# An adaLN transformer block on one core: x's halves on one queue, a first norm in two chains, fill matmuls through the head, and a new issue order

## The chip, the core and the metric

The kernel runs on one core of a Trainium2 chip. A core has engines that each work through their own list of instructions in order: TensorE (PE, matmuls, with the weight loads shown apart as PEld), VectorE (DVE), ScalarE (ACT), GpSimd (POOL), and SyncE (SP), which here only issues transfers. Engines wait for each other by semaphores. The metric is the time of one execution in microseconds (us), lower is better.

## The reference

One transformer block on x of 2048 tokens by 512 features, in bfloat16, with modulation computed from a vector c:

```python
mod = (silu(c) @ w_mod).reshape(1, 6, 1, 512)          # sa, ca, ga, sb, cb, gb
h = layernorm(x) * (1 + ca) + sa
q, k, v = split(h @ wqkv)                              # 32 heads of 16
# token s attends to s, s-2, ..., s-14 (8 keys, positions below 0 masked)
o = softmax(q . k_gathered * 16**-0.5) @ v_gathered
x = x + ga * (o @ wo)
h = layernorm(x) * (1 + cb) + sb
x = x + gb * ((gelu(h @ w_gate) * (h @ w_up)) @ w_down)   # 1792 wide
```

## The kernel before, in words

The tokens are cut into four groups of 512 (`sg` 0 to 3), each of four tiles of 128 tokens on the partitions. For each group: layer norm (`LN1`), transpose to put features on the partitions (`hT`), the projections q, k, v (`qkv`, L562; each is four matmuls of 128 by 128 by 512 into one PSUM buffer, copied out by ScalarE, L576 to L582), the products q times shifted k on VectorE (`pq`, L617), their sums over features by TensorE (`lp`, L631, with a narrow stationary operand), the softmax on VectorE and ScalarE, the products with v (`pv`, L724), their sums (`o`, L738), the output projection (`x1p`, L759) with the residual (L768), the second norm (`LN2`), and the feed-forward part: gate and up (L787), gelu and copy on ScalarE, product on VectorE, and down (`y`, L799). v takes a way through DRAM (`vst`, `V4`), and some transposes go by a transfer (`LN1.3.t`, L463). PSUM has four buffers of the kind `mm`, two of the kind `att` and one for logits. `woS` (L368) and `WdS` multiply the weights wo and w_down by ga and gb on VectorE.

The order of all work is written out by hand as data. Every part of the kernel is a generator that yields steps (`Op`: an engine, a function that emits the instructions, the steps that must come before it, and buffers that it takes and gives). The generators are numbered in the order in which they are started, and the list `ORDER` says whose next step is emitted. So each engine's list of instructions follows `ORDER`; the waits between engines come from the data. The figures inside the steps were used when such a list was made and have no effect on a run.

The head of the kernel is this. x of the first group comes in two halves: tiles 0 and 1 on SP's queue (`x0.0`), tiles 2 and 3 on ScalarE's (`x0.2`, L260). Behind `x0.0` SP issues the weights of the modulation (`wm1`, `wm0`), then `wqkv0`, `x1`, `wqkv1`, `wqkv2`, `x2` and the rest. `mods` computes the modulation: silu of c on ScalarE (L316), a transpose (`scp`, L321), a copy (`scT`), a tiny exp that brings in the exp table (`pre`, L327), and two groups of sixteen matmuls with one column each (`mp1`, `mp0`, L293) whose results ScalarE turns into `scl` and `modT` (`mod1`, `mod0`). `mp3`, `mp4` (for the second norm) and `mp2`, `mp5` (for ga and gb) come later in the same way.

`norm` makes the first norm. Statistics of a tile are either two VectorE instructions (L407, L408; `st`) or, for the tiles in `ACT_CH`, ScalarE's: a copy with accumulation (`sa`, L385), a tiny scaling (`nm`, L391) and a square with accumulation (`sq`, L396). `rst` then adds the epsilon on VectorE (L433 for VectorE's tiles, L438 for ScalarE's) and raises to the power -1/2 on GpSimd (L444, `rs`), and L421 writes the normalized tile (`x0` to `x3`). Group 0 has no tile in `ACT_CH`, and its statistics form two parts (tiles 0 and 1, tiles 2 and 3) inside one generator, which emits all four statistics ahead of the first L421. `transp0` transposes each half on TensorE (`th0`, `th1`, L480), and ScalarE (L513) and VectorE (L511) apply the modulation and write `hT`. `qkv_halves` (L544) makes the first two q projections in halves of 256 tokens.

`warmup` emits twenty matmuls on zeros (L210), whose result nobody reads. In `ORDER` eight stand ahead of `scp`, five between `scp` and `mp1`, and seven between `th1` and the first half of L544.

Of the kernel before, what the change touches and what calls it, by code (L numbers as in the profile page):

```python
# [103 lines left out]
def kernel(  # L104
# [13 lines left out]
    nc = tc.nc  # L118
# [85 lines left out]
    def warmup(cold, n):  # L204
        yield Op("DVE", 0.25, lambda: nc.vector.memset(gB[:], 0.0), fire="warm")
        for k in range(n):
            def f(k=k):
                if k == 0:
                    B["warm"] = T("mm", [P, SG], F32, "warm_ps")
                nc.tensor.matmul(B["warm"][:], lhsT=gB[:, 0:P], rhs=gB[:], start=True, stop=True)  # L210
            yield Op("PE", 0.427 if k < cold else 0.216, f, after=["warm"], take=[SL["mm"]] if k == 0 else [],
                     give=[SL["mm"]] if k == n - 1 else [])

    def loads():
# [43 lines left out]
        def act_q():  # L258
            yield Op("ACT", 0.45, ldc, fire="c", lat=0.0, dma=True)
            yield Op("ACT", 0.46, ldx(0, 2, 4, nc.scalar), fire="x0.2", lat=1.45, dma=True)  # L260

        def sp_q():
            yield Op("SP", 0.47, ldx(0, 0, 2), fire="x0.0", lat=1.0)
            yield Op("SP", 0.47, ldwm(1), take=[SL["h2"]], fire="wm1", lat=3.2)
# [106 lines left out]
    ACT_CH = {"LN1.1": (3, 4), "LN1.2": (2, 4), "LN1.3": (0, 4), "LN2.0": (0, 2), "LN2.1": (0, 4)}  # L371
# [28 lines left out]
    def norm(key, src, ready, ev, parts=((0, 4),)):  # L400
        aa, ab = ACT_CH.get(ev, (0, 0))
        dv = [c4 for c4 in range(CPS) if not aa <= c4 < ab]
        for c4 in dv:
# [6 lines left out]
            for a, b in parts[:-1]:  # L410
                if c4 == b - 1:
                    yield from rst(ev, a, b, [c4 for c4 in dv if a <= c4 < b])
        a, b = parts[-1]
        yield from rst(ev, a, b, [c4 for c4 in dv if a <= c4 < b])
        for c4 in range(CPS):
            def f(c4=c4):
                k = norm_tiles(ev)
                if c4 == 0:
                    B[key] = T("xn", [P, CPS, D], BF16, "xn")
# [3 lines left out]
            yield Op("DVE", 0.325, f, after=[f"{ev}.rs{max(a for a, b in parts if a <= c4)}"],  # L423
# [96 lines left out]
    def ln1(sg):  # L520
        ev = f"LN1.{sg}"
        yield from norm(("xn1", sg), lambda: B["x", sg], lambda c4: [f"x0.{c4 // 2 * 2}"] if sg == 0 else [f"x{sg}"], ev,
                        ((0, 2), (2, 4)) if sg == 0 else ((0, 4),))
        pl.done[ev] = pl.done[f"{ev}.x3"]
# [12 lines left out]
    def qkv_halves():  # L537
        for half in range(2):
# [8 lines left out]
            yield Op("PE", 0.87, f, after=[f"LN1.0.h{d}.{half}" for d in range(DT)] + ["wqkv0"],  # L547
# [329 lines left out]
    pl.spawn(warmup(13, 20))  # L877
# [42 lines left out]
```

## Time and profile before

| | |
|---|---|
| Time, median of 3 runs | 242.76 us |
| Lowest and highest of the runs | 241.57 and 242.9 us |
| Span of the profiled execution, first to last instruction | 240.1 us |
| Whole time of the profiled execution | not given apart from its span |
| Busy: TensorE, VectorE, ScalarE, GpSimd | 233.0, 169.8, 152.8, 15.1 us |
| Moved by transfers | 29.68 MB |
| Mean granted TensorE clock | 0.993 of full |

The profile is a record of one execution: each instruction with its start and duration, the line of the kernel that emitted it, and what ended the idle time before it. Times in it are us from the span's start. "L787 PE MATMUL ... x224" groups the instructions of one line. A row of the chain gives start, duration, engine, tile and line. In a row of a window, each engine's busy time stands in the order TensorE, weight loads, VectorE, ScalarE, GpSimd, with counts in brackets; then the granted clock, the share of the transfer engines, and GB/s. TensorE's matmuls overlap, so its busy time says that it was occupied, not that it ran at its peak.

### The profile page before, as it was taken

How to read it: one execution, taken by the hardware profiler on the slowest of the kernel's cores; microseconds unless marked ns; L12 is line 12 of the kernel's file. 1: busy time of each engine (PE TensorE's matmuls, PEld its weight loads, DVE VectorE, ACT ScalarE, POOL GpSimd, SP SyncE). 2: the span in 40 equal slices, each digit the busy share in tenths (PEclk: the TensorE clock that was granted, in tenths of full speed). 3: DMA queues.
4: the chain of work that ended last, by engine and by line, in shares of the span. 5: the costliest groups of instructions: out<-in, count | busy, mean ns of one | idle time of the engine just before them, and what ended most of it. 6: DMA issues, size and time to landing. Idle time of an engine off the chain costs nothing.

```text
span 240.1 us, 3700 instructions
## 1 busy us (share of the span) xinstructions
PE 233.0 (97%) x1403; PEld 109.5 (46%) x1403; DVE 169.8 (71%) x238; ACT 152.8 (64%) x287; POOL 15.1 (6%) x37
## 2 busy tenths in 40 slices
PE   7799998999999999999999999999999999999994
PEld 2565454443554444444444444444444444444444
DVE  3859899899997998989989897882774212222222
ACT  4469989886998767955557872077356811666400
POOL 3510400300100000100000001000010000000000
PEclk9799999999999999999999999999999999999999
DMA  6997799999935539935201926600104010000011
GB/s 211 349 313 178 220 200 251 308 278 282 198 91 130 176 88 281 198 62 132 83 0 37 210 74 135 124 22 0 46 0 82 7 44 25 22 0 0 0 46 44
DMA packets 35337, 29.68 MB, mean 124 GB/s; under 512 B 12664, under 2 KB 33784, under 8 KB 35320
## 3 DMA queue, kind: packets, MB, share of 16 engines
q1 hardware_dynamic: 35040, 29.19, 49.0%
q8 instruction: 11, 0.18, 0.3%
q10 hardware_dynamic: 280, 0.26, 0.3%
q14 instruction: 6, 0.05, 0.1%
HBM read 22.37 MB, written 4.98 MB: 114 GB/s over the span
## 4 chain that ended last, share of the span: by engine, by line
PE 79%; DVE 13%; POOL 2%; issue 2%; DMA 2%; ACT 0%; ACTq 0%; DVEq 0%
PE u_ps L787 20%; PE g_ps L787 20%; PE y_ps L799 19%; PE x_ps L759 6%; PE qkv_ps L562 5%; DVE pq L617 4%; PE o_ps L738 3%; DVE pv L724 2%; POOL rstd L444 2%; DMA x<-in_A_x_dram 2%; PE LTp L631 2%; DVE xn L421 2%; PE y_ps L810 1%; DVE st L407 1%; PE warm_ps L210 1%
## 5 line engine op out<-in xcount | busy, mean ns | idle before, releaser
L787 PE MATMUL u_ps<-h,Wu 128*128 128x512 bf16 x224 | 57.5, 379 | 0.0
L787 PE MATMUL g_ps<-h,Wg 128*128 128x512 bf16 x224 | 57.5, 379 | 0.0
L827 ACT CAST ub<-u_ps 128x512 bf16<-128x512 f32 x56 | 32.8, 586 | 23.4 <-PE u_ps L787 23.3
L838 DVE TENSOR_TENSOR hht<-gl,ub 128x512 bf16<-128x512 bf16 x56 | 22.8, 420 | 34.5 <-ACT ub L827 34.3
L799 PE MATMUL y_ps<-Wd,hht 128*128 128x512 bf16 x210 | 46.1, 379 | 0.0
L820 ACT ACTIVATE gl<-g_ps 128x512 bf16<-128x512 f32 x56 | 33.6, 600 | 17.7 <-PE g_ps L787 17.3
L562 PE MATMUL qkv_ps<-hT,wqkv 128*128 128x512 bf16 x184 | 41.8, 380 | 0.0
L617 DVE TENSOR_TENSOR pq<-qT,kT 128x4096 bf16<-128x4096 bf16 x16 | 36.2, 2285 | 2.8 <-ACT kT L578 2.8
L724 DVE TENSOR_TENSOR pv<-PT,V 128x4096 bf16<-128x4096 bf16 x16 | 35.9, 2283 | 1.4 <-PE o_ps L738 0.7
L787 PEld LDWEIGHTS <-Wu 128*128 128x128 bf16 x224 | 21.6, 98 | 27.2 <-issue 1.7
L787 PEld LDWEIGHTS <-Wg 128*128 128x128 bf16 x224 | 21.7, 98 | 27.0 <-issue 1.3
L799 PEld LDWEIGHTS <-hht 128*128 128x128 bf16 x210 | 20.6, 98 | 24.8
L562 PEld LDWEIGHTS <-wqkv 128*128 128x128 bf16 x184 | 20.1, 114 | 19.7 <-issue 3.0
L444 POOL TENSOR_TENSOR rstd<-rstd,neghalf 128x4 f32<-128x4 f32 (+1 forms) x9 | 11.4, 1271 | 162.6 <-DVE rstd L438 82.7
L845 DVE TENSOR_TENSOR ot<-y_ps,x 128x512 bf16<-128x512 f32 x15 | 10.1, 686 | 14.0 <-PE y_ps L799 14.0
L495 ACT ACTIVATE h<-h,modT,scl 128x512 bf16<-128x512 bf16 x12 | 8.8, 804 | 12.3 <-DMA h<-xn 12.3
L759 PE MATMUL x_ps<-woP,oT 128*128 128x512 bf16 x64 | 15.5, 379 | 0.0
L407 DVE BATCH_NORM_STATS2 st<-x 128x6 f32<-128x512 bf16 x19 | 12.9, 678 | 3.0 <-DMA x<-in_A_x_dram 3.0
L749 ACT CAST oT<-o_ps 128x512 bf16<-128x512 f32 x16 | 8.7, 587 | 4.7 <-PE o_ps L738 4.7
L768 DVE TENSOR_TENSOR x<-x_ps,x 128x512 bf16<-128x512 f32 x16 | 10.5, 675 | 1.6 <-PE x_ps L759 1.6
L576 ACT CAST qT<-qkv_ps 128x512 bf16<-128x512 f32 x16 | 9.6, 600 | 1.8 <-PE qkv_ps L544 1.2
L578 ACT CAST kT<-qkv_ps 128x512 bf16<-128x512 f32 x16 | 9.7, 609 | 0.8 <-PE qkv_ps L562 0.8
(78 smaller groups left out, 180.8 us busy)
## 6 DMA issues: line engine op xcount, KB each, us to landing
V<-vscr SPq DMA_DIRECT2D x12, 520.0 KB, 9.0
wm<-in_w_mod_dram SPq DMA_DIRECT2D x6, 512.0 KB, 6.7
vscr<-vT SPq DMA_DIRECT2D x4, 512.0 KB, 5.2
out_dram<-ot SPq DMA_DIRECT2D x15, 128.0 KB, 1.7
Wg<-in_B_w_gate_dram SPq DMA_DIRECT2D x1, 1792.0 KB
Wu<-in_B_w_up_dram SPq DMA_DIRECT2D x1, 1792.0 KB
wqkv<-in_A_wqkv_dram SPq DMA_DIRECT2D x3, 512.0 KB, 8.0
x<-in_A_x_dram SPq DMA_DIRECT2D x3, 512.0 KB, 8.8
```

Of the source, the lines that this page charges most:

```text
L407: nc.vector.bn_stats(out=st[:], in_=src()[:, c4, :])
L444: nc.gpsimd.tensor_tensor(out=k["rstd"][:, a:b], in0=k["rstd"][:, a:b], in1=neghalf[:, a:b], op=ALU.pow)
L562: nc.tensor.matmul(ps[:], lhsT=wqkv[blk][:, dt, j::4], rhs=B["hT", sg][:, :, dt, :], start=(dt == 0), stop=(dt == DT - 1))
L617: nc.vector.tensor_tensor(out=pq[:], in0=_ap(B["qT", sg][:, j, :], [[0, W], [1, SG]]), in1=_ap(kT[:, j, sg * SG + 2:sg * SG + 2 + SG], [[2 ...
L724: nc.vector.tensor_tensor(out=t[:], in0=_ap(B["PT", sg][:, 0, :], [[SG, 2], [0, 4], [1, SG]]), in1=_ap(v[:, 0, j, :], [[8, 2], [4 * (SG + ...
L759: nc.tensor.matmul(ps[:], lhsT=B["oT", sg][:, j, c4 * P:(c4 + 1) * P], rhs=woP[:, j, :], start=(j == 0), stop=(j == 3))
L768: nc.vector.tensor_tensor(out=x[:, c4, :], in0=B["x1ps", sg, c4][:], in1=x[:, c4, :], op=ALU.add)
L787: nc.tensor.matmul(ps[:], lhsT=Wt[:, dt, ft * P:(ft + 1) * P], rhs=B["h2T", sg][:, :, dt, :], start=(dt == 0), stop=(dt == DT - 1))
L799: nc.tensor.matmul(ps[:], lhsT=B["hh", sg, ft][:, c4 * P:(c4 + 1) * P], rhs=B["Wd", ft // 4][:, ft % 4, :], start=(ft == 0), stop=(ft == F ...
L820: nc.scalar.activation(out=gl[:], in_=B["g", sg, ft][:], func=ACT.Gelu_apprx_tanh)
L827: nc.scalar.copy(out=ub[:], in_=B["u", sg, ft][:])
L838: nc.vector.tensor_tensor(out=hh[:], in0=B["gl", sg, ft][:], in1=B["ub", sg, ft][:], op=ALU.mult)
```

## The change

It has five parts.

1. `x0.2`, the second half of the first group's x, is issued by SP right behind `x0.0`, ahead of `wm1`, and no longer by ScalarE.
2. The first norm is two generators, `ln1` for tiles 0 and 1 and `ln1b` for tiles 2 and 3; the parameter `parts` of `norm` goes, and `a`, `b` give the range.
3. Tile 1 of the first norm gets its statistics on ScalarE (`"LN1.0": (1, 2)` in `ACT_CH`). In ScalarE's order these three steps stand between silu and `scT`.
4. There are 21 warm matmuls instead of 20. In the new `ORDER` four stand ahead of `scp`, nine between `scp` and `mp1`, four between `mp1` and `mp0`, two between `th0` and `th1` and two between `th1` and L544. The last one fires `warmed`, for which the first half of L544 asks.
5. `ORDER` is new throughout. `ln1b` takes the number 18, so every later number is one higher. Some moves: `mp0` now comes ahead of `th0`; on TensorE `mp4` stands ahead of `qp.1.2.1` (before, behind the transposes of LN1.2); the statistics of LN1.1's tile 3 still stand ahead of the first copy of q on ScalarE; on VectorE `woS` stands behind `pv.0.3` (before, ahead of `pv.0.0`); on SP `Wg` stands behind the LN1.3 transpose and `Wu` behind `V4.1.0`, and `gst2` and `ga` behind group 0's four V loads.

The new head of `ORDER`, up to the first L544 (69th entry, number 21), and the rest of the diff without the remainder of the list:

```diff
 ORDER = [
+    1, 0, 2, 8, 8, 0, 2, 8, 8, 2, 8, 2, 7, 2, 7, 8, 8, 2, 17, 15, 15, 15, 7, 2, 8, 8, 18, 8, 8, 17, 17, 18, 17,
+    2, 8, 8, 7, 8, 7, 8, 17, 18, 8, 18, 8, 7, 8, 7, 2, 17, 18, 0, 19, 18, 7, 9, 8, 14, 20, 8, 19, 20, 14, 2, 3,
+    8, 8, 14, 20, 21, 40, 14, 14, 42, 21, 42, 3, 2, 40, 40, 42, 21, 2, 42, 21, 22, 42, 22, 42, 21, 22, 2, 22,
...
@@ warmup
-                     give=[SL["mm"]] if k == n - 1 else [])
+                     give=[SL["mm"]] if k == n - 1 else [], fire="warmed" if k == n - 1 else None)
@@ loads
         def act_q():
             yield Op("ACT", 0.45, ldc, fire="c", lat=0.0, dma=True)
-            yield Op("ACT", 0.46, ldx(0, 2, 4, nc.scalar), fire="x0.2", lat=1.45, dma=True)
 
         def sp_q():
             yield Op("SP", 0.47, ldx(0, 0, 2), fire="x0.0", lat=1.0)
+            yield Op("SP", 0.47, ldx(0, 2, 4), fire="x0.2", lat=0.75)
...
-    ACT_CH = {"LN1.1": (3, 4), "LN1.2": (2, 4), "LN1.3": (0, 4), "LN2.0": (0, 2), "LN2.1": (0, 4)}
+    ACT_CH = {"LN1.0": (1, 2), "LN1.1": (3, 4), "LN1.2": (2, 4), "LN1.3": (0, 4), "LN2.0": (0, 2), "LN2.1": (0, 4)}
...
-    def norm(key, src, ready, ev, parts=((0, 4),)):
+    def norm(key, src, ready, ev, a=0, b=4):
         aa, ab = ACT_CH.get(ev, (0, 0))
-        dv = [c4 for c4 in range(CPS) if not aa <= c4 < ab]
+        dv = [c4 for c4 in range(a, b) if not aa <= c4 < ab]
...
-            for a, b in parts[:-1]:
-                if c4 == b - 1:
-                    yield from rst(ev, a, b, [c4 for c4 in dv if a <= c4 < b])
-        a, b = parts[-1]
-        yield from rst(ev, a, b, [c4 for c4 in dv if a <= c4 < b])
-        for c4 in range(CPS):
+        yield from rst(ev, a, b, dv)
+        for c4 in range(a, b):
...
-            yield Op("DVE", 0.325, f, after=[f"{ev}.rs{max(a for a, b in parts if a <= c4)}"],
+            yield Op("DVE", 0.325, f, after=[f"{ev}.rs{a}"] + ([f"{ev}.x0"] if c4 else []),
...
-    def ln1(sg):
-        ev = f"LN1.{sg}"
-        yield from norm(("xn1", sg), lambda: B["x", sg], lambda c4: [f"x0.{c4 // 2 * 2}"] if sg == 0 else [f"x{sg}"], ev,
-                        ((0, 2), (2, 4)) if sg == 0 else ((0, 4),))
-        pl.done[ev] = pl.done[f"{ev}.x3"]
+    def x_ready(sg):
+        return lambda c4: [f"x0.{c4 // 2 * 2}"] if sg == 0 else [f"x{sg}"]
+
+    def ln1(sg, a=0, b=4):
+        yield from norm(("xn1", sg), lambda: B["x", sg], x_ready(sg), f"LN1.{sg}", a, b)
...
-            yield Op("PE", 0.87, f, after=[f"LN1.0.h{d}.{half}" for d in range(DT)] + ["wqkv0"],
+            yield Op("PE", 0.87, f, after=[f"LN1.0.h{d}.{half}" for d in range(DT)] + ["wqkv0", "warmed"],
...
-    pl.spawn(warmup(13, 20))
+    pl.spawn(warmup(10, 21))
...
+        for n, g in (("sa1", lambda q: norm_act(lambda: B["x", q], x_ready(q), f"LN1.{q}")),
...
+                     ("ln1", lambda q: ln1(q, 0, 4 if q else 2)), ("ln1b", lambda q: iter(()) if q else ln1(0, 2, 4)),
```

More of the change, by code (lines that the diff above doesn't have):

```diff
@@ L409, in norm @@
             yield Op("DVE", 0.815, f, after=ready(c4), fire=f"{ev}.st{c4}")
-            for a, b in parts[:-1]:
-                if c4 == b - 1:
-                    yield from rst(ev, a, b, [c4 for c4 in dv if a <= c4 < b])
-        a, b = parts[-1]
-        yield from rst(ev, a, b, [c4 for c4 in dv if a <= c4 < b])
-        for c4 in range(CPS):
+        yield from rst(ev, a, b, dv)
+        for c4 in range(a, b):
             def f(c4=c4):
                 k = norm_tiles(ev)
-                if c4 == 0:
+                if key not in B:
                     B[key] = T("xn", [P, CPS, D], BF16, "xn")
@@ L881 @@
     for sg in range(NSG):
-        for n, g in (("sa1", lambda q: norm_act(lambda: B["x", q], lambda c4: [f"x{q}"], f"LN1.{q}")),
-                     ("sa2", lambda q: norm_act(lambda: B["x", q], lambda c4: [f"x1.{q}.{c4}"], f"LN2.{q}")), ("ln1", ln1), ("t1", lambda q: transp(("xn1", q), ("hT", q), "hT", f"LN1.{q}") if q else transp0(("xn1", 0), "LN1.0")), ("h1", lambda q: ln1_ev(q) if q else ln1_ev0(False)), ("qkv", qkv),
+        for n, g in (("sa1", lambda q: norm_act(lambda: B["x", q], x_ready(q), f"LN1.{q}")),
+                     ("sa2", lambda q: norm_act(lambda: B["x", q], lambda c4: [f"x1.{q}.{c4}"], f"LN2.{q}")), ("ln1", lambda q: ln1(q, 0, 4 if q else 2)), ("ln1b", lambda q: iter(()) if q else ln1(0, 2, 4)), ("t1", lambda q: transp(("xn1", q), ("hT", q), "hT", f"LN1.{q}") if q else transp0(("xn1", 0), "LN1.0")), ("h1", lambda q: ln1_ev(q) if q else ln1_ev0(False)), ("qkv", qkv),
                      ("qev", qkv_ev), ("v", vload), ("pq", logits), ("lmm", logits_mm), ("soft", soft), ("ptd", lambda q: pt_dma(q) if q in PT_DMA else iter(())), ("pv", pv), ("pvmm", pv_mm), ("pvev", pv_ev), ("x1mm", x1_mm),
```

62 rows, old and new, of the table ORDER are left out of this document.

## The prediction

> **What bounds the kernel now.** I read the page first, then TensorE's waits, then the chain that ended last, then the first 20 us instruction by instruction. Of the page two lines matter here: the span and the busy time.
>
> ```profile
> span 240.1 us, 3700 instructions
> PE 233.0 (97%) x1403; PEld 109.5 (46%) x1403; DVE 169.8 (71%) x238; ACT 152.8 (64%) x287; POOL 15.1 (6%) x37
> ```
>
> TensorE is busy 97% of the span, though busy includes matmuls that only warm the clock. TensorE's waits (us in total, times, longest) are few; the last row is VectorE's, for later:
>
> ```profile
> PE hTp L480 <- DVE xn L421: 1.5, 1, 1.5
> PE PTp L689 <- DVE e L675: 0.8, 1, 0.8
> PE o_ps L738 <- DVE pv L724: 0.4, 1, 0.4
> DVE xn L421 <- POOL rstd L444: 4.4, 5, 1.2
> ```
>
> The first lies in the head (another, for the memset, stands at the very start). So from the first projection to the end TensorE waits 1.2 us. The chain (start, us, what) shows where that part begins and ends:
>
> ```profile
> 9.85 0.88 PE hTp L480 x8
> 10.72 2.33 PE warm_ps L210 x7
> 13.06 1.75 PE qkv_ps L544 x16
> 17.26 2.29 DVE pq L617
> 61.46 6.16 PE qkv_ps L562 x28
> 71.11 0.86 PE g_ps L787 x4
> 82.69 0.97 PE g_ps L787 x4
> 237.10 0.42 DVE ot L852
> ```
>
> The kernel is a head of 13.06 us and then 224 us of packed TensorE. Less time can come from an earlier L544 only, and only if later waits do not eat it. The head in detail (start, us, engine, line; idle before in brackets):
>
> ```profile
> 3.78 0.70 DVE L407 BATCH_NORM_STATS2 st<-x 128x6 f32<-128x512 bf16 x1 [2.59 <-DMA x<-in_A_x_dram]
> 4.61 0.66 DVE L407 BATCH_NORM_STATS2 st<-x 128x6 f32<-128x512 bf16 x1
> 4.89 1.50 PE L210 MATMUL warm_ps<-gB 128*128 128x512 bf16 x5
> 5.17 1.28 ACT L327 ACT_TABLE_LOAD   x1
> 5.77 0.71 POOL L444 TENSOR_TENSOR rstd<-rstd,neghalf 128x2 f32<-128x2 f32 x1 [3.21 <-DVE rstd L433]
> 6.05 0.70 DVE L407 BATCH_NORM_STATS2 st<-x 128x6 f32<-128x512 bf16 x1 [0.36 <-DMA x<-in_A_x_dram]
> 6.26 0.55 PE L293 MATMUL modT_ps<-scT,wm 128*128 128x1 bf16 x16
> 6.47 0.20 ACT L327 ACTIVATE junk<-neghalf 128x4 f32<-128x4 f32 x1
> 7.87 0.73 DVE L421 TENSOR_SCALAR xn<-x,mv,rstd 128x512 bf16<-128x512 bf16 x2
> 8.04 0.79 POOL L444 TENSOR_TENSOR rstd<-rstd,neghalf 128x2 f32<-128x2 f32 x1 [1.56 <-DVE rstd L433]
> 10.08 1.47 ACT L513 ACTIVATE hT<-hTp,modT,scl 128x256 bf16<-128x256 bf16 x3
> 10.08 1.73 DVE L511 TENSOR_SCALAR hT<-hTp,scl,modT 128x256 bf16<-128x256 bf16 x5 [0.48 <-ACT modT L298]
> 11.44 0.63 ACT L385 ACTIVATE gl<-x 128x512 bf16<-128x512 bf16 x1
> 13.06 0.19 ACT L396 ACTIVATION_READ_ACCUMULATOR gl<-x,sums 128x1 f32 x1
> ```
>
> hT is complete at 10.08+1.73 = 11.81, but seven warm matmuls stand ahead of L544 and hold it to 13.06. They are slow because the clock had fallen, as windows of 1 us show (TensorE busy is the second number, the granted clock follows POOL):
>
> ```profile
> 7.00:8.00 1.00, 0.00 (x0) 0.00 (x0) 0.93 (x4) 0.02 (x1) 0.00 (x0) 1.00 1.08 348
> 9.00:10.00 1.00, 1.00 (x25) 1.00 (x23) 0.60 (x2) 0.12 (x1) 0.74 (x4) 0.50 1.09 347
> ```
>
> **The change, part by part.** *x's second half.* It follows x0.0 on the sync queue and no longer shares the engines with wm1. Before, the third statistic at 6.05 waited for it, the first at 3.78 for x0.0; the loads move 324 GB/s in that microsecond (window 3 to 4), so another 0.26 MB is 0.8 us: 4.6. Bounds: 3.78 and 6.05. At 6.05 the third statistic starts as late as before and about 1.0 us of the gain is lost. I take 4.6. The bytes ahead of wm1 and all later loads stay the same, so these land as before; their issue is later by one issue, about 0.5 us, while their data wait for x anyway. I price that at 0.
>
> ```profile
> 3.00:4.00 1.00, 1.00 (x4) 0.38 (x3) 0.22 (x1) 0.45 (x2) 0.00 (x0) 1.00 0.99 324
> wqkv<-in_A_wqkv_dram SPq DMA_DIRECT2D x1, 512.0 KB, 7.0
> x<-in_A_x_dram SPq DMA_DIRECT2D x1, 512.0 KB, 8.0
> x<-in_A_x_dram SPq DMA_DIRECT2D x1, 512.0 KB, 9.6
> ```
>
> The last three rows (us from issue to landing) are wqkv0, x1 and x2, issued at 2.37, 2.92 and 6.39: landed 9.37, 10.92 and 16.0. wm1 was there at 6.26; wm0 lies between wm1 and wqkv0, so 7.85.
>
> *The norm in two chains.* ScalarE takes the second tile's statistics: from the L385 to the end of the last L396 read it is 13.25-11.44 = 1.81, so 3.78 to 5.59. VectorE does tile 0 (3.78 to 4.6), tile 2 (to 5.45), two tiny adds (to 5.8), tile 3 (to 6.6). The first power runs on GpSimd to 6.6 (0.71), x0 6.65 to 7.0, the second power 7.2 to 8.0 (0.79), x1 to 7.4, x2 and x3 8.0 to 8.75 (0.73). Before, x3 ended at 9.6: 0.85 earlier. The price is that scT, the exp table load and mod1 queue behind the statistics on ScalarE: scT 5.75, table to 7.05, exp to 7.25, mod1 7.45. mod1 waits for nothing else and mod0 is needed later, so 0. If Square needed another table than silu's, 1.28 us would come ahead of it, but the later load would go: bound 0 to 1.28, taken 0 since copies in this trace run under whatever table is in.
>
> [...]
>
> *Fills and the first projection.* There are 21 instead of 20, in front of mp1 (13), between mp1 and mp0 (4), and two each behind th0 and th1. TensorE: 13 warm ones and scp to about 6.4 as before (4.89+1.50), mp1 to 6.9, four fills at full clock (0.216 each) to 7.8, mp0 with wm0 7.85 to 8.3 (mp1's 0.55 at most), th0 to 8.8 (half of the 0.88 that it took at half clock), two fills, th1 9.25 to 9.7, two fills to 10.15. ScalarE gives mod0 8.55, scB 8.75, its two parts of hT (0.49 each) to 9.75; VectorE's two end at 9.55, the last three at 10.75, in time for the second half at 11.0. So L544 starts at **10.15 instead of 13.06: 2.9 us**. The added wait for "warmed" costs nothing in order, since the last fill already stands ahead. wm0's bounds (6.3 and 9.4) move this to 9.9 or 11.6.
>
> *The order anew.* From 10.15 I walked the new order with these durations. ScalarE is full in this stage and TensorE has four PSUM buffers that only ScalarE empties:
>
> ```profile
> 20.00:26.00 6.00, 6.00 (x68) 3.15 (x70) 5.97 (x8) 6.00 (x13) 0.00 (x0) 1.00 0.50 138
> 32.10 1.53 ACT L582 CAST vT<-qkv_ps 128x512 bf16<-128x512 f32 x3
> 51.95 2.93 ACT L495 ACTIVATE hT<-hT,modT,scl 128x512 bf16<-128x512 bf16 x4 [0.47 <-DMA hT<-xn]
> 45.51 8.89 DVE L724 TENSOR_TENSOR pv<-PT,V 128x4096 bf16<-128x4096 bf16 x4
> hT<-xn SPq DMA_TRANSPOSE x1, 6.3
> DMA to landing us min/median/max: 4.9/6.7/8.5
> ```
>
> The x1 statistics stand ahead of the first qT copy on ScalarE and x1 lands no sooner than 10.92, so that copy starts at 12.7 and pq 0 at 14.7 (0.48 a copy). x2 still lands at 16.0 and ScalarE waits for it 0.8 us. TensorE then waits for PSUM at about 28, 34 and 39, some 0.3, 0.8 and 0.3 us. From pq 0 to pv 0 VectorE takes 45.51-17.26 = 28.25 before; woS (L368, 1.2) now stands behind pv, and of the waits for the power (up to 1.2 each) some 1.3 go, since those powers are asked for earlier: 25.7, so pv begins near 40.4. The LN1.3 transpose leaves then and lands 6.3 later, 46.8. Behind it ScalarE has four scalings of hT (0.73) and seven copies of q, k and o (0.49): 6.4, to 53.2, and the first x1 matmul follows at 53.25. From there TensorE has 6 groups of 0.865, two logits groups (1.1 with the switches) to the v projections of group 3: **59.5, where the chain before has 61.46. 1.9 us of the 2.9 remain; 1.0 is lost to ScalarE and PSUM.** Bounds: all 2.9 kept, or nothing.
>
> mp4 (weight-column products) moves ahead of most of group 1's projections. wm4 is issued behind the first v store, about 21.8; with 4.9 to 8.5 us to land it arrives at 26.7 to 30.3, and TensorE asks at 27.4. I take the nearer end, as the queue is half empty then (0.50 share above): 0, with up to 2.6 us in the range. Wg now stands on SP behind the LN1.3 transpose, and Wu behind the second group's first V load, which waits for the buffer that pv frees at 40.4+8.9 = 49.3. Each is 1.8 MB, 5.7 us at 324 GB/s; with the V loads between them both are there by about 60 and read at 69, so 0. If that cover went, TensorE would wait for them outright. gst2 and ga, moved behind V loads on SP, are read by woS alone, near 49.
>
> *From 59.5 on* the matmuls are the same. Two changes between full and quarter-array matmuls fewer, 0.1 each (the 0.97 of the group at 82.69, just behind o_ps, against 0.86), make 0.2 less. VectorE's sum of work ahead of each softmax, pv and y step stands against TensorE's as before or better, so I add no wait but 0.1 for the unforeseen. Sum: -2.9+1.0-0.2+0.1 = **-2.0**: the profiled span goes from 240.1 to 238.1. The median of the runs shown, 242.76, lies 2.66 above that span; with the same around it, **240.7**.
>
> **The rivals.** *The lead is eaten.* ScalarE has 6.00 of 6 us from 20 to 26. If the walk misses another 1 to 2 us of PSUM waits, the kernel comes out at 241.7 to 243.0, about 242.4. Against it: the waits I count have slack on VectorE behind them.
>
> *wm4 holds TensorE (the slower side).* If wm4 lands 9.2 us or more after its issue, TensorE stands until 31 instead of 28 with ten projections behind it, and the time passes 243.97. Landings of 9.6 (x2) exist; with a us more it would be 245. Half a queue free speaks against it. Any other operation put ahead of its load would act alike.
>
> *The clock falls in the head as before.* Between 6.9 and 10.1 TensorE has eight short fills and two single-column groups. At half clock for the 3 us seen before, fills, th1 and L544 take about 1.6 longer: 242.3. Against it stands that no gap over 0.2 is left there, where the gap before L480 was 1.5. [...]
>
> **How the numbers follow.** The forecast has 0.62, eaten lead 0.18, cold clock 0.08, wm4 0.12. The runs spread 241.57 to 242.9, so about 0.5% (1.2 us) can be told from no change. Faster is 0.62, the same 0.18+0.08 = 0.26, slower 0.12. The range is 239.0 (2.9 kept, and most of the 1.2 of later waits gone) to 243.6 (some of wm4); the forecast's own is 239.0 to 241.6.
>
> **What would show it.** L544 starting at 9.9 to 10.7, the second L407 at 4.6 and the third by 5.8, no granted clock under 0.9 between 7 and 12; the first x L385 at 3.8; pq's first at about 14.7; the group 3 v projections near 59.5; u and g by 69.2; TensorE waits of about 2 to 3 us between 24 and 54. Wrong it would be by a first L787 at 71 or later, by modT_ps waiting for wm near 28, or by waits of TensorE after 70.

## The result

| | before | after |
|---|---|---|
| Median of 20 runs each | 242.40 us | 241.11 us |
| Lowest and highest | 240.78 and 243.75 us | 240.08 and 243.78 us |
| Span of the profiled execution | 240.1 us | 238.6 us |
| Ratio of the times, with its 95% interval | | 0.9946 (0.9922 to 0.9970) |

The change makes the kernel 0.54% faster, 1.3 us. The ratio leaves out the longest run of the kernel after (243.78 us), which counts as a slow execution. The forecast was 240.7 us, the range 239.0 to 243.6.

### The profile page after: what moved, and what is told of

It reads as the page before. It is cut to its first block, busy times and chain, and to the rows that moved or that the text cites. A ratio compares the mean times of both kernels' runs of the same rounds, so it can differ in the third digit from the quotient of the medians.

```text
span 238.6 us, 3700 instructions
## 1 busy us (share of the span) xinstructions
PE 231.2 (97%) x1404; PEld 108.7 (46%) x1404; DVE 168.9 (71%) x237; ACT 153.1 (64%) x292; POOL 12.3 (5%) x37
## 4 chain that ended last, share of the span: by engine, by line
PE 85%; DMA 7%; ACT 5%; SPq 1%; issue 0%; DVE 0%
PE g_ps L784 20%; PE u_ps L784 20%; PE y_ps L796 19%; PE qkv_ps L559 10%; DMA wm<-in_w_mod_dram 7%; PE x_ps L756 6%; PE o_ps L735 3%; PE LTp L628 2%; ACT gl L397 1%; PE y_ps L807 1%; ACT gl L386 1%; ACT vT L579 1%; ACT hT L492 1%; PE hTp L454 1%; PE modT_ps L294 0%; ACT kT L575 0%
## 5 line engine op out<-in xcount | busy, mean ns | idle before, releaser
L441 POOL TENSOR_TENSOR rstd<-rstd,neghalf 128x4 f32<-128x4 f32 (+1 forms) x9 | 8.6, 956 | 165.2 <-DVE rstd L435 90.9
L756 PE MATMUL x_ps<-woP,oT 128*128 128x512 bf16 x64 | 16.0, 380 | 0.0
L408 DVE BATCH_NORM_STATS2 st<-x 128x6 f32<-128x512 bf16 x18 | 12.2, 677 | 2.6 <-DMA x<-in_A_x_dram 2.6
L386 ACT ACTIVATE gl<-x 128x512 bf16<-128x512 bf16 x14 | 8.9, 635 | 5.0 <-DVE x L765 3.0
```

What stands on the lines that cost most here:

```text
L386: nc.scalar.activation(out=gpool.tile([P, D], BF16, name="gl")[:], in_=src()[:, c4, :], func=ACT.Copy, accum_out=k["s"][:, 0, c4:c4 + 1])
L408: nc.vector.bn_stats(out=st[:], in_=src()[:, c4, :])
L756: nc.tensor.matmul(ps[:], lhsT=B["oT", sg][:, j, c4 * P:(c4 + 1) * P], rhs=woP[:, j, :], start=(j == 0), stop=(j == 3))
```

## The profile after

The page of the kernel after, its span, the engines' busy time and the granted clock in 40 slices:

```profile
span 238.6 us, 3700 instructions
PE 231.2 (97%) x1404; PEld 108.7 (46%) x1404; DVE 168.9 (71%) x237; ACT 153.1 (64%) x292; POOL 12.3 (5%) x37
PEclk9999999999999999999999999999999999999999
```

In this execution the clock does not fall in the head; in 11 of the 20 runs its mean over the run is 0.991 to 0.993, so it does fall somewhere in them. TensorE's waits (us in total, times, longest), the whole list:

```profile
PE modT_ps L294 <- DMA wm<-in_w_mod_dram: 2.5, 3, 1.4
PE warm_ps L211 <- DVE gB L206: 1.2, 1, 1.2
PE qkv_ps L559 <- ACT vT L579: 0.5, 1, 0.5
```

The wait for the first norm (1.5 us for xn, before), the one for e (0.8) and the one for pv (0.4) are gone. In their place stand three waits for the modulation weights, 2.5 us together. The rows of the head and of mp3 show where (start, us, engine, line; idle before in brackets):

```profile
4.58 0.66 DVE L408 BATCH_NORM_STATS2 st<-x 128x6 f32<-128x512 bf16 x1
5.65 0.69 DVE L408 BATCH_NORM_STATS2 st<-x 128x6 f32<-128x512 bf16 x1
7.19 0.55 PE L294 MATMUL modT_ps<-scT,wm 128*128 128x1 bf16 x16 [0.85 <-DMA wm<-in_w_mod_dram]
7.96 0.74 DVE L418 TENSOR_SCALAR xn<-x,mv,rstd 128x512 bf16<-128x512 bf16 x2 [0.59 <-POOL rstd L441]
8.82 0.55 PE L294 MATMUL modT_ps<-scT,wm 128*128 128x1 bf16 x16 [0.19 <-DMA wm<-in_w_mod_dram]
10.11 0.61 PE L477 MATMUL hTp<-ident,xn 128*128 128x128 bf16 x8
10.99 1.91 PE L541 MATMUL qkv_ps<-hT,wqkv 128*128 128x256 bf16 x16
11.79 0.63 ACT L386 ACTIVATE gl<-x 128x512 bf16<-128x512 bf16 x1 [0.59 <-DMA x<-in_A_x_dram]
15.62 2.29 DVE L614 TENSOR_TENSOR pq<-qT,kT 128x4096 bf16<-128x4096 bf16 x1 [1.07 <-ACT kT L575]
22.55 0.55 PE L294 MATMUL modT_ps<-scT,wm 128*128 128x1 bf16 x16 [1.44 <-DMA wm<-in_w_mod_dram]
```

The norm runs as forecast: the second VectorE statistic at 4.58 and the third at 5.65, the last normalized tile at 7.96+0.74 = 8.70. But wm1 is there only at about 7.1 (before at 6.2; mp1 ran at 6.26), wm0 at 8.8 and x1 at 11.79. The first projection starts at 10.99. In the list by instruction the kernel before has it at 12.89:

```profile
12.89 1.91 PE L544 MATMUL qkv_ps<-hT,wqkv 128*128 128x256 bf16 x16
```

So the head is 1.9 us shorter. The chain of the kernel after shows what becomes of that:

```profile
59.11 6.04 PE qkv_ps L559 x28
69.50 0.86 PE g_ps L784 x4
```

The first gate matmul comes at 69.50 against 71.11 before: 1.6 us of the lead are left, and they stay to the end, since no wait of TensorE follows. From the first projection to the first gate matmul the new order takes 69.50-10.99 = 58.5 us, the old one 71.11-12.89 = 58.2.

Why the loads are late shows in windows of half a microsecond (the last number is GB/s). First before, then after:

```profile
4.00:4.50 0.50, 0.50 (x2) 0.00 (x0) 0.47 (x1) 0.00 (x0) 0.00 (x0) 1.00 1.06 379
4.50:5.00 0.50, 0.50 (x3) 0.21 (x3) 0.49 (x2) 0.01 (x1) 0.00 (x0) 1.00 1.10 389
```

```profile
4.00:4.50 0.50, 0.50 (x3) 0.21 (x2) 0.47 (x2) 0.47 (x2) 0.00 (x0) 1.00 0.67 76
4.50:5.00 0.50, 0.50 (x3) 0.23 (x2) 0.50 (x2) 0.47 (x2) 0.00 (x0) 1.00 0.87 137
```

Between 4 and 5 us, just behind x's second half, the transfers move 0.5*(76+137) = 107 KB where they moved 384 KB before. The 277 KB that are missing are 0.7 us at the rate before. wm1 and x1 come some 0.9 late (6.2 and 10.92 before), and wm0's 8.8 is 0.9 behind the 7.85 of the forecast. The transfer engines do not stand idle for most of this time: the share ahead of the GB/s is 0.67 and 0.87. The packets of that microsecond in the kernel after (number, MB, their time as a share of 16 engines):

```profile
q1 hardware_dynamic: 105, 0.11, 77.2%
```

That is 0.772*16/105 = 0.118 us for a packet of 1 KB. In the kernel before, the same microsecond has 378 packets in 108.0% of the engines' time, 0.046 us each. So the packets behind x's second half are slow, and the engines are idle for about a quarter of the time besides.

## The experiments

Each was timed in five rounds beside the kernel before, in three groups, each group on one chip. Times of different groups are compared only by the ratio to before, and even that with care: one and the same kernel, b_spread, has 0.9875 in group 2 and 0.9913 in group 3. `a_` starts from the kernel after, `b_` from the one before.

| Kernel | Group | Runs | Median us | Before | Ratio (95%) |
|---|---|---|---|---|---|
| after again (a_again) | 1 | 12 | 241.53 | 242.80 | 0.9949 (0.9922 to 0.9976) |
| a_x02_scalar | 1 | 6 | 239.81 | 242.80 | 0.9901 (0.9866 to 0.9936) |
| a_touch | 1 | 9 | 240.38 | 242.80 | 0.9927 (0.9894 to 0.9960) |
| a_mp3_late | 1 | 12 | 240.64 | 242.80 | 0.9928 (0.9903 to 0.9952) |
| a_no_late_fills | 2 | 6 | 241.04 | 243.13 | 0.9911 (0.9883 to 0.9939) |
| b_spread | 2 | 6 | 240.13 | 243.13 | 0.9875 (0.9849 to 0.9901) |
| b_no_late_fills | 2 | 8 | 241.59 | 243.13 | 0.9946 (0.9918 to 0.9974) |
| a_x02_mp3 | 2 | 6 | 239.62 | 243.13 | 0.9857 (0.9824 to 0.9889) |
| after again (a_again2) | 3 | 12 | 240.76 | 242.33 | 0.9946 (0.9924 to 0.9969) |
| a_wm1_scalar | 3 | 6 | 239.75 | 242.33 | 0.9905 (0.9869 to 0.9941) |
| b_spread_again | 3 | 6 | 240.02 | 242.33 | 0.9913 (0.9886 to 0.9940) |
| b_spread_sync | 3 | 12 | 240.75 | 242.33 | 0.9948 (0.9926 to 0.9970) |

**The kernel after again**, no edit.

> The changed kernel once more, to stand beside its variants and for a second profile. In the first profile the clock stayed at 1.0 throughout (mean 1.000); ten of its twenty runs show a mean of 0.991 to 0.993 and are about 1.1 us longer (median 241.4 against 240.3). If the same phase of half clock as in the head of the kernel before lies behind that, a profile with a mean of 0.993 shows 0.50 for about 3.4 us somewhere, and the time is 0.5% under that of the kernel before in either case. If the longer runs come from something else (transfers, a late wait), a profile with 0.993 shows no stretch at half clock within the packed part.

> The changed kernel once more, as the comparison for this call: ratio to before 0.9946 (0.992 to 0.997) as in the two calls so far; wm1 landing at 7.1 to 7.8, TensorE waiting 0.85 to 1.3 for it ahead of mp1, and a mean clock below 0.995 in about half of its executions.

Both ratios repeat the result. The wait ahead of mp1 was 1.08 and 0.52 us in their profiles, and mp3's 2.29 and 1.15: both vary much from run to run. In both profiled executions the clock stayed up, so the question of a_again, where it falls in the other runs of the kernel after, stays open. In a_again2 only 3 of 12 runs were under 0.995, not half.

**Is it the queue of x's second half?** Only that is undone:

```diff
         def act_q():
             yield Op("ACT", 0.45, ldc, fire="c", lat=0.0, dma=True)
+            yield Op("ACT", 0.46, ldx(0, 2, 4, nc.scalar), fire="x0.2", lat=1.45, dma=True)
         def sp_q():
             yield Op("SP", 0.47, ldx(0, 0, 2), fire="x0.0", lat=1.0)
-            yield Op("SP", 0.47, ldx(0, 2, 4), fire="x0.2", lat=0.75)
@@ ORDER
-    1, 0, 2, 8, 8, 0, 2, 8, 8,
+    1, 0, 2, 8, 8, 0, 1, 8, 8,
```

> The changed kernel with x's second half on ScalarE's queue again, nothing else. Theory (the first packets of w_mod are slow for about 1 us, and in the kernel before x's second half filled that time from the other queue): wm1 lands at 6.3 instead of 7.1, wm0 near 7.9 instead of 8.8, x1 at 10.9 instead of 11.8; the third statistic starts at 6.0 instead of 5.65, x3 ends near 9.5, L541 starts at 10.6 to 11.0 against 10.99, and the time is within 0.4 us of the changed kernel. Rival (the dip at 3.5 to 5 us is chance, or comes from the statistics that run then): wm1 lands at 7.1 as well. Second rival (the move of x's half is what brings the gain): L541 starts at 12 or later and the time goes back by 1 us or more.

It is 1.7 us faster than the kernel after beside it (239.81 against 241.53). Its windows, mp1, the first projection, mp3, and the chain:

```profile
4.00:4.50 0.50, 0.50 (x3) 0.20 (x2) 0.50 (x1) 0.50 (x2) 0.00 (x0) 1.00 1.08 383
4.50:5.00 0.50, 0.50 (x3) 0.22 (x2) 0.21 (x2) 0.44 (x3) 0.00 (x0) 1.00 1.08 383
6.91 0.54 PE L293 MATMUL modT_ps<-scT,wm 128*128 128x1 bf16 x16
10.79 1.91 PE L540 MATMUL qkv_ps<-hT,wqkv 128*128 128x256 bf16 x16
21.61 0.55 PE L293 MATMUL modT_ps<-scT,wm 128*128 128x1 bf16 x16 [0.70 <-DMA wm<-in_w_mod_dram]
58.18 6.04 PE qkv_ps L558 x28
```

The transfers run at 383 GB/s through the microsecond of the dip, mp1 waits for no load, and the chain is 0.9 ahead of the kernel after's 59.11, although tile 2 gets its statistics 1.3 later (at 5.93, not 4.58). So this part of the change costs time, 1.7 us where the expectation had at most 0.4. Little of it shows at the first projection, which is 0.2 ahead of the kernel after's (10.79 against 10.99; 11.49 in a_again). The rest is further on: the issues of wm2 and wm3 on SP begin at 9.12 instead of 10.72, wm3 lands at 21.6 instead of 22.5, and mp3 waits 0.70 for it instead of 1.44 (2.29 in a_again). And the mean clock is over 0.995 in all six runs, against 5 of 12 of a_again.

**Does it cost by itself?** The same move (with its entry in `ORDER`), in the kernel before with its late fills spread, beside the kernel it is to be compared with (b_spread, described below, which has the spread fills alone):

```diff
         def act_q():
             yield Op("ACT", 0.45, ldc, fire="c", lat=0.0, dma=True)
-            yield Op("ACT", 0.46, ldx(0, 2, 4, nc.scalar), fire="x0.2", lat=1.45, dma=True)
         def sp_q():
             yield Op("SP", 0.47, ldx(0, 0, 2), fire="x0.0", lat=1.0)
+            yield Op("SP", 0.47, ldx(0, 2, 4), fire="x0.2", lat=0.75)
```

> The kernel before with its last seven fills spread as in b_spread, and with x's second half on the sync queue behind the first, as the change has it; its order is otherwise the old one. Theory A (the move of x's half by itself makes w_mod and what follows late): the third statistic starts at about 4.7 instead of 6.05, but wm1 lands at 7.0 or later (about 6.3 to 6.6 in b_spread), the transfers show a dip below 250 GB/s between 4 and 5 us, TensorE waits 0.5 to 1.5 us ahead of mp1, and the time is 0.5 to 1.5 us longer than that of b_spread_again in this call. Rival B (the move only costs in company with the new order or the norm in two chains): no dip, wm1 by 6.6, and the time equals b_spread_again's within 0.4 us or is shorter, since the last L421 comes up to a microsecond sooner.

```profile
4.00:4.50 0.50, 0.50 (x2) 0.00 (x0) 0.47 (x3) 0.00 (x0) 0.00 (x0) 1.00 0.43 106
8.07 0.58 PE L292 MATMUL modT_ps<-scT,wm 128*128 128x1 bf16 x16 [1.94 <-DMA wm<-in_w_mod_dram]
8.00:9.00 1.00, 0.93 (x18) 0.65 (x19) 0.73 (x2) 0.17 (x1) 0.86 (x5) 0.57 1.07 349
11.00:12.00 1.00, 1.00 (x23) 1.00 (x22) 0.00 (x0) 0.00 (x0) 0.00 (x0) 0.73 1.09 359
```

The dip is there again (106 GB/s), wm1 comes 1.9 us late for mp1, and behind that wait the clock is down from about 8.1 to 11.5 (0.57 and 0.73 granted in the microseconds at the two ends). This execution is the longest of its twelve; in nine of them the clock stayed up. The medians are 240.75 and 240.02, 0.7 us apart, though the intervals of the two ratios overlap a little. The new order and the norm in two chains are not needed for the cost.

**Is the first touch of w_mod slow, or does one queue fall short?** One kernel reads a few bytes of w_mod early (16 KB of columns into a buffer that is written again later, so nothing uses them); the other keeps both halves of x on the sync queue and gives wm1 to ScalarE's queue. Each needs one entry of `ORDER` too:

```diff
# a_touch
             yield Op("ACT", 0.45, ldc, fire="c", lat=0.0, dma=True)
+            yield Op("ACT", 0.45, lambda: nc.scalar.dma_start(
+                out=gR[:, 0, 0:64].rearrange("p (t n) -> p t n", n=16), in_=w_mod[:, D:D + 16].rearrange("(t p) n -> p t n", p=P)), dma=True)
# a_wm1_scalar
             yield Op("ACT", 0.45, ldc, fire="c", lat=0.0, dma=True)
+            yield Op("ACT", 0.46, ldwm(1, nc.scalar), take=[SL["h2"]], fire="wm1", lat=3.2, dma=True)
...
-            yield Op("SP", 0.47, ldwm(1), take=[SL["h2"]], fire="wm1", lat=3.2)
```

> The changed kernel with one tiny load more, ahead of everything else on w_mod: 16 columns of the 512 rows of wm1, issued by ScalarE right behind c, into a tile that is written anew later. Theory (first packets of w_mod are slow, whoever asks): they are slow beside x's transfers, the dip from 3.5 to 5 us goes, wm1 lands at 6.3, wm0 at 7.9, x1 at 11.0, L541 starts at 10.1 to 10.4 and the time is 0.6 to 0.9 us less than the changed kernel's. Rival (the dip comes from the queue running dry behind x, or from the statistics that run at that time): the dip stays and the time is the same, or 0.2 more for ScalarE's issue.

> The changed kernel with wm1 issued by ScalarE's queue behind c, and both halves of x still on the sync queue. Theory A1 (one queue alone doesn't keep the transfer engines fed in the first microseconds): with two queues the dip between 4 and 5 us is gone (over 300 GB/s in each half microsecond), wm1 lands by 6.8, TensorE's wait ahead of mp1 is under 0.3, and the time is about 1 us below a_again2's. Rival A2 (the first bytes of w_mod behind x's are slow whichever queue asks): the dip stays, wm1 lands at 7.1 or later and the time is a_again2's within 0.4. Either way x0.2 may land later than 4.6, by up to 1 us, since wm1 now shares the engines with it.

a_touch first, one window and mp1:

```profile
4.00:4.50 0.50, 0.50 (x3) 0.19 (x2) 0.47 (x2) 0.47 (x3) 0.00 (x0) 1.00 0.98 286
7.65 0.55 PE L295 MATMUL modT_ps<-scT,wm 128*128 128x1 bf16 x16 [0.57 <-DMA wm<-in_w_mod_dram]
```

The dip is shallower, but wm1 is as late as ever and the chain no earlier (59.42 against 59.11), so an early touch does not bring the load in time. The times do not fit this so well: 240.38 is 1.2 us under a_again, in the direction of the theory, with the clock over 0.995 in all nine runs. Why is not known; a slow first touch is not borne out by the loads, and not ruled out either. Then a_wm1_scalar:

```profile
4.00:4.50 0.50, 0.50 (x3) 0.20 (x2) 0.47 (x2) 0.47 (x3) 0.00 (x0) 1.00 1.08 381
6.37 0.54 PE L293 MATMUL modT_ps<-scT,wm 128*128 128x1 bf16 x16
10.12 1.91 PE L540 MATMUL qkv_ps<-hT,wqkv 128*128 128x256 bf16 x16
21.90 0.55 PE L293 MATMUL modT_ps<-scT,wm 128*128 128x1 bf16 x16 [1.66 <-DMA wm<-in_w_mod_dram]
22.00:23.00 1.00, 1.00 (x18) 0.58 (x18) 1.00 (x1) 0.46 (x1) 0.00 (x0) 0.67 0.70 220
23.00:25.00 2.00, 2.00 (x15) 1.11 (x17) 0.71 (x2) 0.58 (x1) 0.00 (x0) 0.50 0.95 277
25.00:26.00 1.00, 1.00 (x17) 0.37 (x20) 1.00 (x1) 0.92 (x2) 0.00 (x0) 0.63 0.95 327
```

With a second queue at work the dip is gone (381), wm1 is in time at 6.37, and the first projection starts at 10.12. The time is 1.0 us below the kernel after beside it, with six runs and intervals that overlap. So in these microseconds the transfers kept their rate where two queues asked at once, whichever load stood on the second: from 4.0 to 4.5 us five profiles with x's halves and wm1 on one queue (after, a_again, a_again2, a_mp3_late, b_spread_sync) have 70 to 225 GB/s, five with x's second half or wm1 on ScalarE's queue (before, b_spread, b_spread_again, a_x02_scalar, a_wm1_scalar) 309 to 385. Only part of the delay can be the later issue: SP issues wm1 at 1.81 with x's half ahead of it and at 1.32 without, half a microsecond, where wm1 comes 0.9 late. What makes the packets of the one queue slow was not found.

The same run shows the next wait. mp3 now stands 1.66 us for wm3, and in the profiled execution, the longest of the six, the clock fell behind that, from 22.3 to 25.7.

**What does mp3 ahead of its load cost?** In the new order mp3 stands on TensorE ahead of group 0's last k projection, the second transpose of LN1.1 and the first sums of `lp`; here it, its copy and wm4's load come behind the first of these sums:

```diff
@@ ORDER (the generator numbered 10 makes mp3, the one numbered 3 issues wm3 and wm4)
-    44, 22, 10, 45, 23, 21, 45, 24, 3, 44, 22, 45, 45, 90, 10, 25, 25, 9, 24, 25,
+    44, 22, 45, 23, 21, 45, 24, 44, 22, 45, 45, 90, 25, 10, 3, 25, 9, 10, 24, 25,
```

> The changed kernel with mp3 (and its copy, and wm4's load, which needs mp3's buffer) moved behind the projection 1.3, the second transposes of LN1.1 and the first logits sum. In the changed kernel TensorE waits 1.44 us at 21.1 for wm3. Theory (TensorE's waits count one for one): that wait goes, the 59.97 at which the v projections of group 3 start becomes 58.6 to 59.2, and the time is 0.8 to 1.4 us less than the changed kernel's. Rival (ScalarE and VectorE are as full as TensorE in this stage): waits for PSUM or for pq take its place, and the time is within 0.3 us.

```profile
23.00 0.55 PE L293 MATMUL modT_ps<-scT,wm 128*128 128x1 bf16 x16
PE qkv_ps L558 <- ACT qT L572: 0.4, 1, 0.4
PE LTp L627 <- DVE pq L613: 0.3, 1, 0.3
58.65 6.04 PE qkv_ps L558 x28
```

mp3 waits for no load any more. Two other waits, 0.7 together, take half of the 1.44 us back, and the chain is 0.5 ahead of the kernel after. The medians are 0.9 us apart (240.64 and 241.53), but part of that is the clock, which is over 0.995 in 9 of 12 runs against 5 of 12. The intervals (0.9903 to 0.9952 against 0.9922 to 0.9976 of a_again) overlap: a gain of some tenths, its size not settled by the times.

**What are the fills worth?** Three kernels. b_spread moves the last seven fills of the kernel before (they stood between th1 and L544): five go behind mp1, two behind mp0. b_no_late_fills drops the seven. a_no_late_fills drops the eight behind mp1 from the kernel after. The last two lose the entries in `ORDER` too.

```diff
# b_spread: ORDER, generator 8 makes the fills
-    7, 7, 7, 17, 17, 17, 18, 7, 7, 17, 17, 18, 7, 14, 19, 19, 0, 8, 8, 8, 8, 8, 19, 8, 8, 14, 14,
+    7, 7, 7, 8, 8, 8, 8, 8, 17, 17, 17, 18, 7, 7, 8, 8, 17, 17, 18, 7, 14, 19, 19, 0, 19, 14, 14,
# b_no_late_fills
-    pl.spawn(warmup(13, 20))
+    pl.spawn(warmup(13, 13))
# a_no_late_fills
-    pl.spawn(warmup(10, 21))
+    pl.spawn(warmup(10, 13))
```

> The kernel before with its own twenty warm matmuls, the last seven placed anew: five behind mp1 and two behind mp0, none behind the second half's transposes. Nothing else is changed. Theory (the changed kernel's gain is the clock): the idle 6.8 to 8.3 us is filled, the granted clock stays at 1.0 in most runs, L544 starts at 11.0 to 11.8 instead of 13.06, and the time is 240.0 to 240.9, so 0.7% to 1.1% under the kernel before and no worse than the changed kernel. Rival (the gain is the norm's two chains and the new order): L544 comes earlier but the time stays within 0.3% of the kernel before.

> The kernel before with its last seven fills spread (five behind mp1, two behind mp0), once more beside the others of this call. Its ratio to the kernel before was 0.9875 (0.9849 to 0.9901) on another chip; the theory that the fills alone carry the gain expects 0.985 to 0.990 again, the L543 start at 10.6 to 11.1 and no granted clock below 0.95 after 4 us. [...]

> The kernel before without its last seven warm matmuls. Theory (real matmuls bring the clock up as warm ones do, so that those seven only hold L544 back): L544 starts at 10.9 to 11.8 at half clock and ends by 13.4 to 14.2 where it ended at 14.80; the time is 0.6 to 1.4 us less than the kernel before's, the mean clock the same 0.993. Rival (without them the clock comes up later): half clock lasts to 14 us or beyond, L544 ends at 14.8 or later, and the time is the same or up to 1 us more.

> The changed kernel with 13 warm matmuls: the eight behind mp1 (four ahead of mp0, two behind each half's transposes) are left out. Theory (their worth is the clock): TensorE idles between mp1 and mp0 and between the transposes, the granted clock falls to 0.50 from about 9 us for some 3.4 us in nearly every run (mean 0.993, as in most runs of the kernel before; the changed kernel has it in about half of its runs), and the median is 0.5 to 1.2 us above the changed kernel's. Rival (the fills only fill): L541 starts up to 0.4 us earlier, at 10.6, the clock is as often 1.0 as in the changed kernel, and the time is the same or 0.4 less.

b_spread, its clock (after GpSimd's busy time), first projection and chain:

```profile
9.00:12.00 3.00, 2.82 (x43) 2.37 (x40) 2.77 (x8) 2.21 (x6) 1.97 (x10) 1.00 1.10 349
11.02 1.80 PE L543 MATMUL qkv_ps<-hT,wqkv 128*128 128x256 bf16 x15 [0.18 <-ACT hT L512]
59.55 6.16 PE qkv_ps L561 x28
```

The old order with the old norm and both queues, and the fills alone moved, starts L543 at 10.57 (its first matmul) and 11.02 (the other fifteen), as early as the changed kernel. The chain is 1.9 ahead of before's 61.46. The time is 3.0 us less in group 2 and 2.3 in group 3, at least as much as the whole change gains. In group 3, beside the kernel after, it is 0.7 us faster than that. Its ratio there, 0.9913, lies just above the 0.985 to 0.990 that the theory had expected, but the clock was up in all six runs as in group 2. The record gives both groups the same chip number, 7. b_no_late_fills:

```profile
9.00:12.00 3.00, 2.92 (x36) 2.35 (x36) 2.48 (x8) 1.91 (x5) 2.08 (x11) 0.53 1.09 348
10.87 2.85 PE L543 MATMUL qkv_ps<-hT,wqkv 128*128 128x256 bf16 x16
60.38 6.17 PE qkv_ps L561 x28
```

Without the seven the clock falls as before, and the projections themselves are slow (2.85 for 1.91), yet the kernel is 1.5 us faster than before. Where the seven stood they did nothing but hold L544. By this, 1.5 of the 3.0 us that b_spread gains in the same group come from no longer holding it, and the other 1.5 from the clock that stays up. Last a_no_late_fills:

```profile
9.00:15.00 6.00, 5.92 (x49) 4.68 (x50) 4.15 (x12) 4.30 (x12) 1.10 (x5) 0.50 1.10 350
11.20 3.62 PE L540 MATMUL qkv_ps<-hT,wqkv 128*128 128x256 bf16 x16
59.88 6.04 PE qkv_ps L558 x28
```

Half clock from 9 to 15: the sixteen matmuls take 3.62 instead of 1.91. But the chain is only 0.8 behind the kernel after: TensorE comes later to mp3 and no longer waits for its load, where the kernel after waits 1.44. The clock fell in all six runs, as the theory had it, but the loss of 0.5 to 1.2 us that it expected does not show: the ratio, 0.9911, is no worse than the kernel after's in the other groups. The kernel after was not timed in this group, and b_spread beside it is 0.9 us faster. So in the new order no worth of the eight late fills is shown.

**The two repairs together.** a_x02_mp3 has x's half on ScalarE's queue and mp3 put back; the rest is the kernel after.

> The changed kernel with both mends: x's second half on ScalarE's queue and mp3 with wm4's load moved back. Theory (the two costs stand in different places and add): clock 1.0 in all runs as with x's half alone, no wait for wm1, none for wm3 (0.7 us there with x's half alone), the time 0.3 to 0.7 us under that of x's half alone (239.8), so 239.1 to 239.5. Rival (the wait for wm3 has slack behind it, as the smaller step of mp3 alone suggests): PSUM waits take its place and the time stays within 0.2 us of 239.8.

```profile
23.09 0.55 PE L293 MATMUL modT_ps<-scT,wm 128*128 128x1 bf16 x16
57.80 6.04 PE qkv_ps L558 x28
```

No wait for a load of w_mod is left, and the chain is 1.3 ahead of the kernel after. At 0.9857 it has the best ratio, 3.5 us under the kernel before. Whether the two repairs add is not shown: x's half alone was timed in another group, where its median was 239.81, 0.2 above this one's 239.62. b_spread in the same group is 0.5 us behind it; by that the new order and the norm in two chains are worth some 0.5 us, which the intervals don't tell from nothing. The other such pair, a_wm1_scalar and b_spread_again, has 239.75 and 240.02.

## Why the prediction was right, and where its steps failed

The sign and about the size were right, the terms less so. Forecast was a span of 238.1 from -2.9 (head), +1.0 (lost to ScalarE and PSUM), -0.2 and +0.1. Measured is 238.6 from -1.9 in the head, +0.3 from there to the first gate matmul and +0.1 behind it, in an execution with the clock up. That the total came so near is in part luck: the head fell short by 1.0 us, and the loss behind it was 0.7 smaller than forecast, for another reason than the one named. The step from span to time was loose too. Each run's time is 2.0 us above its own span (240.59 and 238.6), so the 2.66 us that the forecast added hold 0.7 by which the profiled execution before happened to be quicker than the median of three runs; and 238.1+2.66 is 240.76, which it gave as 240.7.

*What held.* x's half at 4.6 (4.58), the third statistic by 5.8 (5.65), the last L418 ending at 8.75 (8.70). Behind the table load the next activation starts at once, as the forecast counted: the load ends at 5.62+1.28 = 6.90, and the activation starts at 6.91.

```profile
5.62 1.28 ACT L328 ACT_TABLE_LOAD   x1
6.91 0.21 ACT L328 ACTIVATE junk<-neghalf 128x4 f32<-128x4 f32 x1
```

wm4 held nobody, and TensorE waits for nothing after 70. Group 3's v projections start at 59.11 (59.5). Other signs came out late: L541 at 10.99 (9.9 to 10.7), the first pq at 15.62 (14.7), the first gate matmul at 69.50 (69.2).

*The step that failed* reads: "The bytes ahead of wm1 and all later loads stay the same, so these land as before; their issue is later by one issue, about 0.5 us, while their data wait for x anyway. I price that at 0." They wait for more than x: behind x's half the transfers move 107 KB in a microsecond where they moved 384. wm1 is 0.9 late, and with it mp1, mod1, mp0, th0 and th1, to L541 at 10.99 instead of 10.15. That the rest of that walk was right, a_wm1_scalar shows: with wm1 in time the first projection starts at 10.12. What the step cost is the 0.7 us of b_spread_sync and the 1.7 of a_x02_scalar; in the latter the shorter wait at mp3 and the clock that stays up have their share.

*The lost lead was over-sized.* Of TensorE's waits for PSUM at 28, 34 and 39 only one came (0.5 at 36). Instead mp3 waits 1.44 for wm3 at 22.5. The forecast looked at mp4's load and not at mp3's, and said only that any other operation put ahead of its load would act alike. Part of this wait is the late loads once more, since it is 0.70 with x's half on ScalarE's queue. Taking it away gains only some 0.5 us in the chain (a_mp3_late). In all, the stretch up to the first gate matmul gives back 0.3 us, not 1.0.

*The clock had too small a chance.* "No gap over 0.2 is left there", the forecast said; with wm1 late there is one of 0.5 to 1.3 us. The mean granted clock of each run tells how it went. Over 0.995 it was in 23 of the 44 runs of the kernel after, in 3 of the 62 of the kernel before in the three groups, and in all 12 of b_spread. In the first comparison the runs of the kernel after have a median of 240.3 with the clock up and 241.4 with a mean of 0.991 to 0.993. So the rival of the falling clock, given 0.08, is true of about half of the executions, at 1.1 us rather than 1.6, and the median lies between the two. (In a_again the two kinds of run are only 0.2 us apart, in a_again2 1.0.) Whether it falls in the head, as the rival had it, is not shown: no run of the kernel after with a fallen clock was profiled. The one gap of that length in the head is ahead of mp1; mp3's wait is another place, where a_wm1_scalar lost it.

*What the change is made of*, then: taking the block of fills from ahead of L544 and spreading it is worth 2.3 to 3.0 us (b_spread), half of that by not holding L544; x's move to one queue takes back 0.7 to 1.7; and the order with the norm in two chains is worth 0.3 to 0.5 us in the two pairs that show it, neither told from nothing. How that splits between the order and the norm, no run shows. The 0.85 us that the forecast gained at the last L421 gave little by itself: TensorE stood behind its own fills before, and stands behind wm1 now. With wm1 in time (a_wm1_scalar) the first projection does start at 10.12, against 10.57 for the first matmul of L543 in b_spread and 11.02 for the other fifteen.

## What to carry to other kernels

Fill matmuls belong where TensorE would stand idle, one gap at a time, and not in a block ahead of the first real work, which they hold up (spreading the block gained 2.3 to 3.0 us here); try first what the kernel does without them, which was half of the gain here (1.5 of 3.0 us). In the first microseconds of this kernel, moving a load from a second queue to the first slowed the transfers (107 KB from 4 to 5 us, 384 KB before) although the bytes stay the same, so the load behind it is to be priced by its own landing, not by the sum of bytes. For each operation that moves ahead in an order, look up when its own load lands; one forgotten (mp3) was a wait of 1.4 us, of which some 0.5 reached the chain.

## What the runs showed of the hardware that was not expected

*The clock fell for 3.4 us, and in one profile for twice that.* Each time half clock is read from the windows' shares. In b_spread_sync 0.57 in 8 to 9 is 0.86 us at half clock, then 2.0, then 0.73 in 11 to 12 is 0.54: 3.40. In a_wm1_scalar it is 0.66+2.0+0.74 = 3.40. The mean of 0.993 over 238.6 us is 3.3 us. In a_no_late_fills (0.79 in 8 to 9, 0.50 from 9 to 15, 0.80 in 15 to 16) it is 0.42+6.0+0.40 = 6.82, twice as long. The length of the wait ahead did not decide it: the clock fell behind waits of 1.94 (b_spread_sync) and 1.66 us (a_wm1_scalar), and did not behind one of 2.29 (mp3 in a_again). What decides it was not shown. The clock came up again without fills as well: in b_no_late_fills, where none stands behind mp1, the shares from 9 to 13 us (0.59, 0.50, 0.50, 0.71) give 3.40 too.

*A second queue does more here than save the time of an issue.* The issue of x's second half takes SP 0.5 us, and wm1's delay is 0.9 in the kernel after, with 76 and 137 GB/s where two queues move 379 and 389 (before), and with 0.118 us for a packet of 1 KB where they take 0.046. In a_again packets are less slow and engines more idle (225 and 231 GB/s at shares of 0.66 and 0.69), so the two come in different shares. This is measured at one place, the first transfers of a run; later in the kernel nothing of the kind was looked at.
